# One-core local attention with an MLP on Trainium2: later buffers for the attention and new durations in its list schedule

## The chip, the cores and the metric

The kernel runs as one program on one core of a Trainium2 chip. The metric is the device time of one execution in microseconds. Engines are named as the profile names them: PE is TensorE (matmuls; PEld its weight loads), DVE is VectorE, ACT is ScalarE, POOL is GpSimd, SP is the engine whose queue issues every DMA here.

## The reference

```
q, k, v: (4, 8, 768, 64) float32
k_sum, v_sum = max over blocks of 32 of k, mean over blocks of 32 of v
scores = [ (q k^T)/8 where |i - j| < 16, else -1e9  |  (q k_sum^T)/8 + log 32 ]
a = exp(scores - rowmax); a = a / (sum + 1e-9)
attn = a @ [v | v_sum]                     (4, 8, 768, 64)
x = heads side by side                     (4, 768, 512)
xn = layernorm(x) * g_ln
out = x + relu(xn @ w_ch1) @ w_ch2         512 -> 2048 -> 512
```

## The kernel before

**The work.** The 3072 rows are 24 tiles of 128 (T); each tile's heads are two halves, so attention has 48 steps, t = 0 to 47, and the MLP works on 12 groups of two tiles (g). The first 12 steps (batch 0) run in float32 from K and V held whole on chip (tiles `k0_0` to `k0_3`, `qw0` to `qw5`, `vw0` to `vw5`; each step copies its window of K to `kx0` or `kx1`). The other 36 are "late" steps, in pairs of float16 numbers: `load_q` and `load_k` (lines 539 to 565) fetch q and the two halves of K (`ksg`), POOL puts the 24 block maxima beside the window, ACT makes the high half (`qhl`, `kh`) and DVE the low half (`kl`); `qk` multiplies on PE (`s`); `softmax` runs on DVE, POOL and ACT; `transp` (line 623) splits the probabilities (`p16`) and has a DMA transpose them (`pT`); `pv` multiplies with V on PE (`o`). Then `ln` and `lnT` normalize a tile and put it transposed into `xs`.

For each later batch, `batch_k`, `batch_q`, `batch_v` and `batch_s` read all of K, Q and V once more in pieces (staging tiles `bst`; in batch 1 `bst` and `qs` in turn) for maxima, sums and scales.

**The MLP.** The weights arrive as 32 pieces of 512 KB (`raw`); `dec_w` rebuilds each in three DVE operations (`wf`, `wf`, `raw`) and takes its squares on ACT, `scale_w` finds a scale from four or eight of them, `conv_w` splits each piece into a high half (ACT) and a low one (DVE), `wp`. Then `g1` (96 blocks, `h`, 24 matmuls each of 256 columns, read out by ACT as `hh` and by DVE as `hl`; two PSUM buffers for `h`) and `g2` (`a`, 512 columns).

**What sets the order.** Nothing is issued while the program is described. `Plan.record` keeps every operation with what it must follow; `Plan.schedule` is a list schedule over five in-order engines that uses a table of durations (`Plan.cost`), of waits between engines (`WAIT`, plus `slack`, a margin for some waits) and a simple model of the DMA queue; `Plan.improve` runs it forwards and backwards 32 times and keeps the order with the earliest end. `Plan.issue` then emits the operations in that order, all from one line, so every row of the profile says L321. Each engine runs its own list strictly in order, SP too: a DMA that must wait holds up all behind it.

**Buffers.** `work` gives a tile by its tag; a tag with one buffer must be let go by its last reader before the next tile of that tag is written. Before, `ksg` has one buffer (tag `qke`), `kh` one for each half, `qs`, `p16`, `pT` and `bst` one each. Two lines that the steps touch:

```python
ksg = work("qke", f"ksg{t}_{pr}", [P, 2, NC])
WAIT = dict(tensor=200, vector=140, scalar=160, gpsimd=90, sync=940)
```

Of the kernel before, what the change touches and what calls it, by code (L numbers as in the profile page):

```python
# [15 lines left out]
F16 = mybir.dt.float16  # L16
# [5 lines left out]
B, H, S, D = 4, 8, 768, 64  # L22
DM, DFF = 512, 2048
P = 128
# [5 lines left out]
NC = 184  # L30
# [25 lines left out]
LOADS = [("fetch_k0", 0), ("fetch_k0", 1), ("fetch_q", 0), ("gain",), ("fetch_blocks",), ("fetch_k0", 2), ("fetch_k0", 3)]  # L56
LOADS += [("fetch_v0", c) for c in range(7)] + [("fetch_tail", 0), ("fetch_q", 1), ("fetch_tail", 1), ("fetch_tail", 2)]
NV = 3
SLACK = 2500
SLACK2 = 800  # L60
WORDER = (
# [25 lines left out]
class Plan:  # L87
# [1 line left out]


    ENGINES = ("tensor", "vector", "scalar", "gpsimd", "sync")
    WAIT = dict(tensor=200, vector=140, scalar=160, gpsimd=90, sync=940)
    SAME = dict(tensor=0, vector=127, scalar=143, gpsimd=100, sync=0)
    ISSUE, SETUP, TICK, SWITCH, FIRST = 450, 650, 10240 / 3, 93, 3500

    def __init__(self):
        self.ops, self.slots, self.prev, self.uses = [], {}, {}, {}
        self.joined = False
        self.stages, self.stage = {None: 0}, 0
        for e in self.ENGINES:  # L100
            setattr(self, e, Plan.Queue(self, e))

# [7 lines left out]
    def step(self, f):  # L110


        def call(*a):
            outer, self.stage = self.stage, self.stages.setdefault((f.__name__, a), len(self.stages))
            f(*a)
            self.stage = outer

        return call
# [66 lines left out]
    def cost(self, engine, op, a, k, ins, outs):  # L185

        free = lambda x: math.prod(n for _, n in x.ap[1:])
        n = max(free(x) for x in ins + outs) if engine != "tensor" else free(a[0])
        if engine == "sync":
            x = (outs + ins)[0]  # L190
            return self.ISSUE, x.ap[0][1] * free(x) * mybir.dt.size(x.dtype) / (200.0 if "transpose" in op else 360.0)
        if engine == "tensor":
            dt = ins[-1].dtype
            if dt == F32R:
                return 0.443 * max(n, 256) + 4.5, 0.0
            if dt == F16 or op == "transpose":
                return max((1 if dt == F16 else 2) * n / 2.4 + 3.0, 28.0), 0.0
            return (2 if ins[0].ap[0][1] > D else 1) * max(2 * n / 2.4 + 2.0, 100.0), 0.0
        psum = any(x.space == bass.MemoryType.PSUM for x in ins)
        pointers = sum(1 for x in ins[1:] if free(x) == 1)  # L200
        if engine == "scalar":
            extra = ("accum_out" in k) + sum(isinstance(k.get(x), bass.AP) for x in ("scale", "bias"))
            return n / 1.2 + (51 if psum else 93) + 93 * extra, 0.0
        if engine == "vector":
            fixed = {"transpose": 183, "tensor_tensor_reduce": 158}.get(op, 70)
            return n / (1.92 if op == "tensor_scalar" and not psum else 0.96) + fixed + 61 * (pointers > 0), 0.0
        if op == "tensor_scalar":
            return 180 + n + 61 * pointers + 300 * (n == 1), 0.0
        if op == "tensor_copy":
            return 120 + 3.33 * n, 0.0  # L210
        if op == "tensor_tensor":
            shifted = outs[0].offset // outs[0].ap[0][0] != ins[0].offset // ins[0].ap[0][0]
            return 517 if n == 1 else 40 + 2.1 * n + 110 * (shifted or outs[0].dtype == F32R), 0.0
        return 60 + 0.8 * n, 0.0
# [7 lines left out]
        return engine == "vector" and (len(on_sbuf) > 1 or op == "tensor_scalar" and len(on_sbuf) == 1)  # L222

    def waits(self, x):
        e = [self.ops[j].engine for j in x.after]
        late = self.slack(x)
        return [(j, self.SAME[a] * y if a == x.engine else self.WAIT[a] + late) for a, (j, y) in zip(e, x.after.items())]

    def slack(self, x):

        name, a = self.names[x.stage]
        if x.engine != "tensor" or not a:
            return 0.0
        return SLACK * (name in ("qk", "pv", "batch_s")) + SLACK2 * (name in ("g1", "g2") and a[0] >= 24)

    def schedule(self, rank, after, back):

        count = len(self.ops)
        before = [[] for _ in range(count)]
        left = [len(x) for x in after]  # L240
        for i, x in enumerate(after):
            for j, wait in x:
                before[j].append((i, wait))
        ready, start, end = [0.0] * count, [0.0] * count, [0.0] * count
        free = dict.fromkeys(self.ENGINES, 0.0)
        coming, waiting = ({e: [] for e in self.ENGINES} for _ in range(2))
        ring, warm, columns, tick = 0.0 if back else self.FIRST, False, 0.0, 0.0
        port, half = 0.0, 0
        for i in range(count):
            if not left[i]:  # L250
                heapq.heappush(coming[self.ops[i].engine], (0.0 if back else 1000.0, i))
        for _ in range(count):
            t, e = min(
                (free[e] if waiting[e] else max(free[e], coming[e][0][0]), k)
                for k, e in enumerate(self.ENGINES)
                if waiting[e] or coming[e]
            )
# [12 lines left out]
            if e == "tensor" and not back:  # L270
                while t >= tick + self.TICK:
                    warm, columns, tick = columns >= 3200, 0.0, tick + self.TICK
                busy *= 1 if warm else 2
                at, per = t, self.ops[i].columns / busy
                while t + busy >= tick + self.TICK:
                    columns += (tick + self.TICK - at) * per
                    warm, columns, tick = columns >= 3200, 0.0, tick + self.TICK
                    at = tick
                columns += (t + busy - at) * per
            start[i], free[e], end[i] = t, t + busy, t + busy  # L280
            if e == "sync":
                ring = max(ring, t if back else t + busy + self.SETUP) + moving
                if back:
                    free[e] = max(free[e], ring)
                end[i] = ring + (self.SETUP + busy if back else 0)
            for j, wait in before[i]:
                ready[j] = max(ready[j], end[i] + wait)
                left[j] -= 1
                if not left[j]:
                    heapq.heappush(coming[self.ops[j].engine], (ready[j], j))  # L290
        return start, end
# [10 lines left out]
        return best  # L302

    def issue(self, nc):
        self.names = {n: k or ("", (0,)) for k, n in self.stages.items()}
        for x in self.ops:
            x.first = in_front(self.names[x.stage], x.engine)
        after = [self.waits(x) for x in self.ops]
# [5 lines left out]
        for i in reversed(range(len(after))):  # L314
            x = self.ops[i]
# [10 lines left out]
def body(ctx: ExitStack, tc, qt, qa, qe, kt, ks, va, vb, vs, g_ln, w1, w2, blocks, out):  # L326
# [5 lines left out]
    def work(tag, name, shape, dt=F32, bufs=1):  # L332
        return pl.tile(wp, shape, dt, tag, name, bufs)
# [23 lines left out]
    late = {}  # L357
# [41 lines left out]
    def go_late():  # L399
        nc.gpsimd.memset(prob[0][:, :, NC:], 0.0)  # L400
        for i in range(2):
            t = late["v", i] = work(f"v16_{i}", f"v16_{i}", [P, 2, 4, 2, D], F16)
            nc.gpsimd.memset(t[:], 0.0)

    stg_n = [0]

    def stg(tag, shape, dt=F32):
        stg_n[0] += 1
        if tag == "bst1":
            tag = ("bst", "qs")[stg_n[0] % 2]  # L410
        return work(tag, f"{tag}{stg_n[0]}", shape, dt, 1 + (tag == "xn"))


# [138 lines left out]
    def load_k(t, pr):  # L552
        T, hh = divmod(t, 2)
        b = T // NT
        ksg = work("qke", f"ksg{t}_{pr}", [P, 2, NC])
        nc.sync.dma_start(ksg[:], kt[T, hh, pr])
        nc.gpsimd.tensor_copy(
            ksg[:, :, 160 : 160 + NB], bt["k", b][:, 2 * hh + pr]
        )
        kh = work(f"kh{pr}", f"kh{t}_{pr}", [P, 2, NC], F16)  # L560
        kl = work("kl", f"kl{t}_{pr}", [P, 2, NC], F16, 2)
        sc = bt["s", b][:, 2:3]
        nc.scalar.activation(kh[:], ksg[:], AF.Copy, scale=sc)
# [59 lines left out]
    def transp(t):  # L623

        p = st[t, "p"]
        p16 = work("p2", f"p16_{t}", [P, 4, 3, P], F16)
        first, rest, last = (p16[:, :, i] for i in range(3))
        nc.scalar.copy(first, p[:, :, :P])
        nc.scalar.copy(last[:, :, :D], p[:, :, P:])
        nc.gpsimd.tensor_tensor(rest, p[:, :, :P], first, ALU.subtract)  # L630
        nc.gpsimd.tensor_tensor(last[:, :, D:], p[:, :, P:], last[:, :, :D], ALU.subtract)
        pT = work("pta", f"pT_{t}", [P, 12, P], F16)
# [440 lines left out]
```

## Time and profile before

| | |
|---|---|
| runs | 643.06, 643.38 and 646.51 us; median 643.38 us |
| the profiled execution | 640.14 us, of which 638.4 us from its first to its last instruction |
| PE busy | 609.2 us of 638.4 (95%), mean granted clock 0.989 |
| DVE, ACT, POOL busy | 454.4 (71%), 391.2 (61%), 198.7 us (31%) |
| DMA | 93.14 MB; the one queue's packets take 55.3% of 16 engines' span |

PE is in use nearly throughout, so what PE does not do (its idle time and the stretches at a lower granted clock) is all that an order can win. The sum of idle PE is 638.4 - 609.2 = 29.2 us; where it lies is read from a table by stretch, and what it waited for from the waits of that stretch.

### The profile page before, as it was taken

How to read it: one execution, taken by the hardware profiler on the slowest of the kernel's cores; microseconds unless marked ns; L12 is line 12 of the kernel's file. 1: busy time of each engine (PE TensorE's matmuls, PEld its weight loads, DVE VectorE, ACT ScalarE, POOL GpSimd, SP SyncE). 2: the span in 40 equal slices, each digit the busy share in tenths (PEclk: the TensorE clock that was granted, in tenths of full speed). 3: DMA queues.
4: the chain of work that ended last, by engine and by line, in shares of the span. 5: the costliest groups of instructions: out<-in, count | busy, mean ns of one | idle time of the engine just before them, and what ended most of it. 6: DMA issues, size and time to landing. Idle time of an engine off the chain costs nothing.

```text
span 638.4 us, 13412 instructions
## 1 busy us (share of the span) xinstructions
PE 609.2 (95%) x4611; PEld 430.7 (67%) x4611; DVE 454.4 (71%) x1190; ACT 391.2 (61%) x1036; POOL 198.7 (31%) x412
## 2 busy tenths in 40 slices
PE   8967999999989999899999999999999999999997
PEld 6845766664666776676676677776776766666665
DVE  4899989899678797677776788578776875432212
ACT  4989899678477775658667576565656664210100
POOL 5122110133343352363333545344344443200000
PEclk9979899999999999999999999999999999999999
DMA  9972476525967856678675675456665453420000
GB/s 287 351 270 70 128 260 213 192 83 124 237 162 179 194 138 162 174 160 195 176 145 149 152 170 114 111 132 150 153 147 140 113 149 75 62 51 1 17 16 34
DMA packets 124996, 93.14 MB, mean 146 GB/s; under 512 B 84864, under 2 KB 107392, under 8 KB 124928
## 3 DMA queue, kind: packets, MB, share of 16 engines
q1 hardware_dynamic: 124928, 92.29, 55.3%
q8 instruction: 36, 0.59, 0.4%
q14 instruction: 32, 0.26, 0.1%
HBM read 66.27 MB, written 6.29 MB: 114 GB/s over the span
## 4 chain that ended last, share of the span: by engine, by line
PE 42%; DVE 21%; DMA 20%; ACT 8%; issue 5%; SPq 2%; POOL 2%; ACTq 0%; POOLq 0%; DVEq 0%
PE h L321 19%; PE a L321 19%; DMA raw<-in_w 6%; DMA ksg<-in_kt 5%; DMA bst<-in_vs 4%; ACT p L321 3%; DVE p L321 2%; DVE wp L321 2%; DVE x L321 2%; DVE kl L321 2%; SPq L321 2%; DVE hl L321 2%; DMA bst<-in_ks 2%; PE s L321 2%; DVE wf L321 2%
## 5 line engine op out<-in xcount | busy, mean ns | idle before, releaser
L321 PE MATMUL h<-xs,wp 128*128 128x256 f16 x2304 | 274.8, 275 | 8.5 <-DVE hl L321 6.5
L321 PEld LDWEIGHTS <-wp 128*128 128x128 f16 x2304 | 225.5, 99 | 51.5 <-issue 8.6
L321 PE MATMUL a<-wp,hh 128*128 128x512 f16 (+1 forms) x768 | 226.7, 377 | 1.0 <-ACT hh L321 0.9
L321 PE MATMUL a<-wp,hl 128*128 128x512 f16 x384 | 144.9, 377 | 0.1
L321 PEld LDWEIGHTS <-hh 128*128 128x128 f16 x784 | 75.6, 98 | 68.0 <-ACT hh L321 1.1
L321 ACT ACTIVATE hh<-h 128x512 f16<-128x512 f32 x96 | 55.8, 584 | 88.6 <-PE h L321 88.2
L321 DVE SCALAR_TENSOR_TENSOR hl<-h,hh 128x512 f16<-128x512 f32 x96 | 65.3, 683 | 62.1 <-ACT hh L321 61.6
L321 ACT ACTIVATE p<-p,mn,sv 128x184 f32<-128x184 f32 x144 | 76.2, 530 | 22.2 <-POOL mn L321 21.7
L321 POOL TENSOR_TENSOR p<-p,p 128x512 f16<-128x512 f32 x72 | 70.1, 988 | 32.3 <-ACT p L321 32.1
L321 DVE SCALAR_TENSOR_TENSOR kl<-ksg,sv,kh 128x368 f16<-128x368 f32 x72 | 48.4, 672 | 30.9 <-ACT kh L321 30.8
L321 ACT ACTIVATE kh<-ksg,sv 128x368 f16<-128x368 f32 x72 | 42.9, 596 | 42.8 <-POOL ksg L321 37.2
L321 PEld LDWEIGHTS <-hl 128*128 128x128 f16 x392 | 38.3, 98 | 45.1 <-DVE hl L321 0.6
L321 ACT ACTIVATE bst<-bst 128x384 f32<-128x384 f32 (+2 forms) x55 | 32.3, 588 | 32.1 <-DVE vsum L321 15.1
L321 POOL TENSOR_SCALAR mn<-mn,sv 128x2 f32<-128x2 f32 x72 | 33.5, 466 | 56.0 <-DVE mn L321 55.6
L321 POOL COPY ksg<-ksum 128x48 f32<-128x48 f32 x72 | 19.1, 265 | 97.4 <-DMA ksg<-in_kt 90.0
L321 DVE SCALAR_TENSOR_TENSOR x<-a,wsc,x 128x512 f32<-128x512 f32 (+1 forms) x48 | 35.4, 737 | 18.4 <-PE a L321 18.3
L321 DVE CUSTOM_DVE_ANT_0 p<-s,mask 128x184 f32<-128x184 f32 x144 | 43.3, 340 | 1.4 <-PE s L321 1.4
L321 DVE SCALAR_TENSOR_TENSOR v<-vst,sv,v 128x256 f16<-128x256 f32 x72 | 36.6, 533 | 3.2 <-ACT v L321 2.9
L321 ACT CAST p<-p 128x512 f16<-128x512 f32 x72 | 33.9, 504 | 8.0 <-DMA pT<-p 7.7
L321 POOL TENSOR_TENSOR x<-x,rc 128x256 f32<-128x256 f32 x36 | 25.7, 715 | 40.5 <-DVE x L321 39.4
L321 ACT ACTIVATE v<-vst,sv 128x512 f16<-128x512 f32 x36 | 25.5, 712 | 11.5 <-PE o L321 11.5
L321 DVE SCALAR_TENSOR_TENSOR qhl<-qs,sv,qhl 64x512 f16<-64x512 f32 x36 | 28.2, 785 | 4.0 <-ACT qhl L321 2.9
(118 smaller groups left out, 767.6 us busy)
## 6 DMA issues: line engine op xcount, KB each, us to landing
raw<-in_w SPq DMA_DIRECT2D x32, 512.0 KB
ksg<-in_kt SPq DMA_DIRECT2D x72, 184.0 KB
qs<-in_qt SPq DMA_DIRECT2D x72, 128.0 KB
out_x<-x SPq DMA_DIRECT2D x23, 256.0 KB
vst<-in_va SPq DMA_DIRECT2D x36, 128.0 KB
bst<-in_ks SPq DMA_DIRECT2D x20, 192.0 KB
bst<-in_qa SPq DMA_DIRECT2D x15, 256.0 KB
bst<-in_vs SPq DMA_DIRECT2D x20, 192.0 KB
```

The costliest lines, as they stand in the source:

```text
L321: getattr(getattr(nc, self.ops[i].engine), op)(*a, **k)
```

## The change

Three things. **Homes:** late attention's tiles take tags in turn from a list, `HOMES`; the added tags are those of tiles that batch 0 is the last to use. `ksg` has three places in place of one, `kh` four in place of two, `qs`, `p16`, `pT` and `bst` two in place of one. **Durations:** the table gives a DMA's issue time by kind of step, a longer wait for its landing by kind of step, and other constants for several DVE, ACT, POOL and PE operations. **Margins:** `SLACK2` 800 becomes 1500 ns, and waits of ACT, DVE, POOL and SP in late attention get 1000 ns on what a DMA brings and 150 ns on the rest. Cut to its core:

```diff
+HOMES = dict(
+    ksg=("qke", "k0_0", "k0_1"),
+    kh=("kh0", "kh1", "kx0", "kx1"),
+    qs=("qs", "qw0"),
+    p16=("p2", "k0_2"),
+    pT=("pta", "k0_3"),
+    bst=("bst", "qw1"),
+)
-SLACK2 = 800
+SLACK2 = 1500
+SLACKD, SLACKE, LATE = 1000, 150, 14
...
-    ISSUE, SETUP, TICK, SWITCH, FIRST = 450, 650, 10240 / 3, 93, 3500
+    SETUP, TICK, SWITCH, FIRST = 1100, 10240 / 3, 93, 3500
+    ISSUE = dict(transp=1550, lnT=1250, batch_vput=760, load_q=500)
+    LAND |= dict(batch_q=1350, batch_v=1300, load_q=1350, load_v=1150, transp=1050)
...
-            return self.ISSUE, x.ap[0][1] * free(x) * mybir.dt.size(x.dtype) / (200.0 if "transpose" in op else 360.0)
+            return self.ISSUE.get(self.names[self.stage][0], 380), x.ap[0][1] * free(x) * mybir.dt.size(x.dtype) / (200.0 if "transpose" in op else 360.0)
...
+                wait.append((j, self.slack(x, y) + (self.LAND.get(n, 1000) if y.engine == "sync" else self.WAIT[y.engine])))
...
+        late = name in ("load_q", "load_k", "load_v", "softmax", "transp", "pv") and a[0] >= LATE
+        late |= name[:5] == "batch" and a[0] >= 2
+        late |= name in ("ln", "lnT") and a[0] >= LATE // 2
+        late |= name in ("g1", "g2") and a[0] >= 24
+        if not late:
             return 0.0
+        return SLACKD if y.engine == "sync" else SLACKE
...
-                ring = max(ring, t if back else t + busy + self.SETUP) + moving
+                ring = max(ring, t if back else t + self.SETUP) + moving
...
+    def home(kind):
+        n = turn[kind] = turn.get(kind, -1) + 1
+        return HOMES[kind][n % len(HOMES[kind])]
...
-        ksg = work("qke", f"ksg{t}_{pr}", [P, 2, NC])
+        ksg = work(home("ksg"), f"ksg{t}_{pr}", [P, 2, NC])
...
-        kh = work(f"kh{pr}", f"kh{t}_{pr}", [P, 2, NC], F16)
+        kh = work(home("kh"), f"kh{t}_{pr}", [P, 2, NC], F16)
```

No operation is added or taken away; their order changes on every engine. (The numbers after a name: `ksg20_0` is step 20, half 0; the last number is a running one.) Three places.

SP, where the K loads of steps 20 and 21 stand. Before:

```order
L321 DMA ksg20_0_688<-in_kt 128x368
L321 DMA_TRANSPOSE pT_18_633<-p16_18_632 128x12x128
L321 DMA vst1_78<-in_vb 32x256
L321 DMA vst1_78<-in_va 128x256
L321 DMA vst1_78<-in_vb 32x256
L321 DMA bst63_728<-in_vs 96x512
L321 DMA ksg20_1_691<-in_kt 128x368
L321 DMA qs66_755<-in_qt 64x512 x2
L321 DMA bst82_1051<-in_ks 128x384
L321 DMA ksg21_0_735<-in_kt 128x368
```

And of the change:

```order
L349 DMA ksg20_0_688<-in_kt 128x368
L349 DMA vst1_78<-in_vb 32x256
L349 DMA vst0_77<-in_vb 32x256
L349 DMA qw064_733<-in_qt 64x512 x2
L349 DMA qw161_726<-in_vs 96x512
L349 DMA ksg20_1_691<-in_kt 128x368
L349 DMA_TRANSPOSE pT_17_611<-p16_17_610 128x12x128
L349 DMA ksg21_0_735<-in_kt 128x368
L349 DMA vst0_77<-in_vb 32x256
L349 DMA_TRANSPOSE xs3_513<-x16_6_514 128x8x128
```

The load of `ksg20_0` stood beside the transpose of step 18 and now stands beside that of step 16; the loads run further ahead of the rest of attention.

ACT, from the read-out of block 24 of `g1` to that of block 26. Before:

```order
L321 ACTIVATE hh24_554<-h24_553 128x512
L321 ACTIVATE p_88,sum18_631<-p_88,mn18_630,sv1_435 128x184 x4
L321 CAST p16_18_632<-p_88 128x4x128
L321 CAST p16_18_632<-p_88 128x4x64
L321 ACTIVATE kh19_1_643<-ksg19_1_642,sv1_435 128x368
L321 ACTIVATE bst61_726,vabs2_704<-bst61_726 96x512
L321 ACTIVATE hh25_559<-h25_558 128x512
L321 ACTIVATE v16_1_262<-vst1_78,sv1_435 128x8x64
L321 ACTIVATE hh26_562<-h26_561 128x512
```

And of the change:

```order
L349 ACTIVATE hh24_554<-h24_553 128x512
L349 CAST p16_19_649<-p_88 128x4x128
L349 CAST p16_19_649<-p_88 128x4x64
L349 ACTIVATE bst62_727,vabs2_704<-bst62_727 96x512
L349 ACTIVATE qw163_728,vabs2_704<-qw163_728 96x512
L349 ACTIVATE kh21_1_739<-ksg21_1_738,sv1_435 128x368
L349 ACTIVATE hh25_559<-h25_558 128x512
L349 ACTIVATE qhl22_756<-qs66_755,sv1_435 128x512
L349 ACTIVATE v16_0_261<-vst0_77,sv1_435 128x8x64
L349 ACTIVATE kh22_0_758<-ksg22_0_757,sv1_435 128x368
L349 ACTIVATE p_88,sum20_697<-p_88,mn20_696,sv1_435 128x184 x3
L349 ACTIVATE hh26_562<-h26_561 128x512
```

The softmax beside these blocks was that of step 18 and is that of step 20; the K and q work is that of steps 21 and 22 where it was step 19. By block 47 this has grown: before, the `qk` of 16 steps (14 to 29) stand on PE between blocks 16 and 47 of `g1`; now 19 steps (14 to 32).

ACT, around the read-outs of blocks 2 and 3, early in the kernel (`tx3` is a transpose on PE whose copy, `xs1`, all of blocks 8 to 15 need). Before:

```order
L321 ACTIVATE hh2_302<-h2_301 128x512
L321 ACTIVATE bst10_414,vabs1_407<-bst10_414 128x384
L321 CAST xs1_191<-tx3_218 128x512
L321 ACTIVATE wf13_312,wacc_81<-raw13_276 128x512
L321 ACTIVATE wf14_313,wacc_81<-raw14_277 128x512
L321 ACTIVATE wf15_314,wacc_81<-raw15_278 128x512
L321 ACTIVATE hh3_305<-h3_304 128x512
```

And of the change:

```order
L349 ACTIVATE hh2_302<-h2_301 128x512
L349 ACTIVATE bst8_412,vabs1_407<-bst8_412 128x384
L349 ACTIVATE hh3_305<-h3_304 128x512
L349 CAST xs1_191<-tx3_218 128x512
L349 ACTIVATE qs9_413,vabs1_407<-qs9_413 128x384
L349 ACTIVATE bst10_414,vabs1_407<-bst10_414 128x384
L349 ACTIVATE wf16_342,wacc_81<-raw16_299,gcol_74 128x512
```

The copy of `tx3` was two rows behind `hh2` and ahead of `hh3`, and now follows `hh3`: on PE the transpose `tx3` stood between blocks 2 and 3, and now comes after block 3, directly ahead of a small scale matmul and block 8 (before, step 8's `qk` and block 9 came next).

## Rows read from the trace of the kernel before

**Rows 1.** The page, part 1: busy us (share of the span) and instructions of each engine.
```profile
PE 609.2 (95%) x4611; PEld 430.7 (67%) x4611; DVE 454.4 (71%) x1190; ACT 391.2 (61%) x1036; POOL 198.7 (31%) x412
```

**Rows 2.** Busy time by stretch: us, busy (count) by engine, granted clock, DMA share, GB/s.
```profile
32.00:64.00 32.00, 21.44 (x146) 16.91 (x143) 30.64 (x87) 28.42 (x92) 7.84 (x19) 0.85 0.49 171
64.00:96.00 32.00, 31.12 (x234) 23.63 (x233) 30.01 (x85) 29.55 (x90) 4.68 (x14) 0.94 0.62 194
...
160.00:192.00 32.00, 28.78 (x246) 21.31 (x245) 21.36 (x52) 19.82 (x50) 12.19 (x22) 1.00 0.76 198
192.00:256.00 64.00, 63.56 (x498) 44.02 (x497) 53.72 (x145) 44.12 (x115) 23.88 (x47) 1.00 0.71 169
256.00:320.00 64.00, 60.44 (x475) 42.12 (x474) 45.85 (x114) 42.95 (x115) 26.70 (x52) 1.00 0.72 176
320.00:384.00 64.00, 61.53 (x492) 44.19 (x491) 49.36 (x135) 43.00 (x109) 25.70 (x48) 1.00 0.66 154
384.00:512.00 128.00, 128.00 (x1053) 93.70 (x1052) 97.31 (x253) 80.97 (x196) 55.18 (x97) 1.00 0.58 134
```

**Rows 3.** Waits of PE, 160 to 384 us: us in total, times, longest.
```profile
PE h L321 <- DVE hl L321: 4.5, 5, 1.2
PE s L321 <- DVE kl L321: 1.9, 4, 0.7
PE h L321 <- DMA xs<-x: 1.5, 2, 0.8
PE a L321 <- ACT hh L321: 0.9, 1, 0.9
```

**Rows 4.** Waits of all engines in the same stretch.
```profile
POOL ksg L321 <- DMA ksg<-in_kt: 56.2, 30, 5.5
...
DVE vsum L321 <- DMA bst<-in_vs: 9.7, 8, 2.8
```

**Rows 5.** Waits of SP's queue in the same stretch.
```profile
SPq L321 <- DVE kl L321: 18.6, 16, 2.2
SPq L321 <- ACT bst L321: 16.6, 14, 3.9
```

**Rows 6.** Timeline of SP, 240 to 300 us: start, us, instruction.
```profile
239.66 1.66 SPq L321 DMA_TRANSPOSE pT<-p  x1
...
253.97 0.33 SPq L321 DMA_DIRECT2D ksg<-in_kt  x1
...
294.40 0.52 SPq L321 DMA_DIRECT2D ksg<-in_kt  x1
...
297.94 2.05 SPq L321 DMA_TRANSPOSE pT<-p  x1
```

**Rows 7.** Timeline of POOL, the same stretch; in brackets the idle time before.
```profile
256.36 0.53 POOL L321 COPY ksg<-ksum 128x48 f32<-128x48 f32 x1 [0.65 <-DMA ksg<-in_kt]
...
298.19 0.22 POOL L321 COPY ksg<-ksum 128x48 f32<-128x48 f32 x1 [1.67 <-DMA ksg<-in_kt]
```

**Rows 8.** Timeline of DVE, 28 to 64 us.
```profile
45.39 1.88 DVE L321 SCALAR_TENSOR_TENSOR raw<-raw,wf 128x512 uint32<-128x512 uint32 x3
47.19 0.54 DVE L321 TENSOR_REDUCE kmax<-bst 128x12 f32<-128x384 f32 x1
```

**Rows 9.** Timeline of PE, 42 to 76 us; in brackets the idle time before.
```profile
50.50 0.88 PE L321 MATMUL pp<-ident,p 128*128 128x128 f32 x3 [1.60 <-ACT p L321]
...
62.91 5.15 PE L321 MATMUL h<-xs,wp 128*128 128x256 f16 x24
68.03 0.63 PE L321 MATMUL tx<-ident,xn 128*128 128x128 f32 x4
68.50 2.78 PE L321 MATMUL h<-xs,wp 128*128 128x256 f16 x24
...
73.14 1.47 PE L321 MATMUL h<-xs,wp 128*128 128x256 f16 x12 [0.52 <-DVE wsc L321]
```

**Rows 10.** Timeline of DVE, 66 to 72 us.
```profile
70.67 0.68 DVE L321 TENSOR_TENSOR xs<-tx,xs 128x512 f16<-128x512 f32 x1
```

More of the change, by code (lines that the diff above doesn't have):

```diff
@@ L91 @@
     ENGINES = ("tensor", "vector", "scalar", "gpsimd", "sync")
-    WAIT = dict(tensor=200, vector=140, scalar=160, gpsimd=90, sync=940)
+    WAIT = dict(tensor=200, vector=140, scalar=160, gpsimd=90, sync=1000)
     SAME = dict(tensor=0, vector=127, scalar=143, gpsimd=100, sync=0)
-    ISSUE, SETUP, TICK, SWITCH, FIRST = 450, 650, 10240 / 3, 93, 3500
+    SETUP, TICK, SWITCH, FIRST = 1100, 10240 / 3, 93, 3500
+    ISSUE = dict(transp=1550, lnT=1250, batch_vput=760, load_q=500)
+    LAND = dict(fetch_v0=2050, fetch_k0=1950, fetch_q=2000, fetch_w=1750, fetch_tail=2000, gain=2000)
+    LAND |= dict(batch_q=1350, batch_v=1300, load_q=1350, load_v=1150, transp=1050)
     def __init__(self):
@@ L98, in __init__ @@
         self.joined = False
-        self.stages, self.stage = {None: 0}, 0
+        self.names, self.stage = [("", ())], 0
         for e in self.ENGINES:
@@ L113, in call @@
         def call(*a):
-            outer, self.stage = self.stage, self.stages.setdefault((f.__name__, a), len(self.stages))
+            outer, self.stage = self.stage, len(self.names)
+            self.names.append((f.__name__, a))
             f(*a)
@@ L197, in cost @@
                 return max((1 if dt == F16 else 2) * n / 2.4 + 3.0, 28.0), 0.0
-            return (2 if ins[0].ap[0][1] > D else 1) * max(2 * n / 2.4 + 2.0, 100.0), 0.0
+            return max(2 * n / 2.4 + 2.0, 100.0) * 2 if ins[0].ap[0][1] > D else 2 * n / 2.4 + 53.0, 0.0
         psum = any(x.space == bass.MemoryType.PSUM for x in ins)
@@ L202, in cost @@
             extra = ("accum_out" in k) + sum(isinstance(k.get(x), bass.AP) for x in ("scale", "bias"))
-            return n / 1.2 + (51 if psum else 93) + 93 * extra, 0.0
+            weights = self.names[self.stage][0] in ("dec_w", "conv_w")
+            return n / 1.2 + (51 if psum else 93) + 93 * extra + 35 * weights, 0.0
         if engine == "vector":
-            fixed = {"transpose": 183, "tensor_tensor_reduce": 158}.get(op, 70)
-            return n / (1.92 if op == "tensor_scalar" and not psum else 0.96) + fixed + 61 * (pointers > 0), 0.0
+            fixed = {"tensor_tensor_reduce": 78, "reciprocal": 90}.get(op, 70) + 61 * pointers
+            fixed += 119 * (self.box(ins[0])[1] == D)
+            return n / (1.92 if op == "tensor_scalar" and not psum else 0.96) + fixed, 0.0
         if op == "tensor_scalar":
-            return 180 + n + 61 * pointers + 300 * (n == 1), 0.0
+            return 180 + n + 61 * pointers + 90 * (n == 1), 0.0
         if op == "tensor_copy":
-            return 120 + 3.33 * n, 0.0
+            return 60 + 3.33 * n, 0.0
         if op == "tensor_tensor":
@@ L224, in waits, with slack @@
     def waits(self, x):
[L225 to L229, printed above, removed]
-        name, a = self.names[x.stage]
-        if x.engine != "tensor" or not a:
+        wait = []
+        for j, real in x.after.items():
+            y = self.ops[j]
+            if y.engine == x.engine:
+                wait.append((j, self.SAME[x.engine] * real if x.engine != "sync" or real else None))
+            else:
+                n = self.names[y.stage][0]
+                wait.append((j, self.slack(x, y) + (self.LAND.get(n, 1000) if y.engine == "sync" else self.WAIT[y.engine])))
+        return wait
+    def slack(self, x, y):
+        name, a = self.names[x.stage]
+        if x.engine == "tensor":
+            if name in ("g1", "g2"):
+                return SLACK2 * (a[0] >= 24)
+            return SLACK * (name in ("qk", "pv", "batch_s"))
+        late = name in ("load_q", "load_k", "load_v", "softmax", "transp", "pv") and a[0] >= LATE
[3 more added lines that the diff above has]
+        if not late:
             return 0.0
-        return SLACK * (name in ("qk", "pv", "batch_s")) + SLACK2 * (name in ("g1", "g2") and a[0] >= 24)
+        return SLACKD if y.engine == "sync" else SLACKE
     def schedule(self, rank, after, back):
@@ L281, in schedule @@
             if e == "sync":
-                ring = max(ring, t if back else t + busy + self.SETUP) + moving
+                ring = max(ring, t if back else t + self.SETUP) + moving
                 if back:
                     free[e] = max(free[e], ring)
-                end[i] = ring + (self.SETUP + busy if back else 0)
+                end[i] = ring + (self.SETUP if back else 0)
             for j, wait in before[i]:
-                ready[j] = max(ready[j], end[i] + wait)
+                ready[j] = max(ready[j], free[e] if wait is None else end[i] + wait)
                 left[j] -= 1
@@ L304, in issue @@
     def issue(self, nc):
-        self.names = {n: k or ("", (0,)) for k, n in self.stages.items()}
         for x in self.ops:
@@ L403, in go_late @@
             nc.gpsimd.memset(t[:], 0.0)
+    turn = {}
+    def home(kind):
+        n = turn[kind] = turn.get(kind, -1) + 1
+        return HOMES[kind][n % len(HOMES[kind])]
     stg_n = [0]
@@ L410, in stg @@
             tag = ("bst", "qs")[stg_n[0] % 2]
+        elif tag in ("bst", "qs"):
+            tag = home(tag)
         return work(tag, f"{tag}{stg_n[0]}", shape, dt, 1 + (tag == "xn"))
@@ L625, in transp @@
         p = st[t, "p"]
-        p16 = work("p2", f"p16_{t}", [P, 4, 3, P], F16)
+        p16 = work(home("p16"), f"p16_{t}", [P, 4, 3, P], F16)
         first, rest, last = (p16[:, :, i] for i in range(3))
@@ L631, in transp @@
         nc.gpsimd.tensor_tensor(last[:, :, D:], p[:, :, P:], last[:, :, :D], ALU.subtract)
-        pT = work("pta", f"pT_{t}", [P, 12, P], F16)
+        pT = work(home("pT"), f"pT_{t}", [P, 12, P], F16)
         nc.sync.dma_start_transpose(pT[:], p16.rearrange("p j i k -> p (j i k)"))
```

## The prediction

> **What bounds the kernel now.** I began with the busy shares: PE works 609.2 us of the span of 638.4 [rows 1], so nothing but the 29.2 us of idle PE, and time at a lower granted clock, can be won by an order. The table by stretch then says where they lie [rows 2]. Idle PE is the stretch less PE's busy time: 10.56 us in 32 to 64, 0.88 in 64 to 96; then 3.22, 0.44, 3.56 and 2.47 in the four stretches from 160 to 384, together 9.69; and none in 384 to 512. The reader should see two different limits. Up to 96 us DVE is busy 30.64 and 30.01 of 32 us: it rebuilds and splits the weights, PE waits for it, and the granted clock is 0.85 and 0.94. From 160 to 384 us no engine but PE is full (DVE 45.85 of 64 in 256 to 320) and the clock is 1.00; PE still stops.
>
> What it stops for is in its waits of that stretch [rows 3]: low halves of the MLP (`h` for `hl`) 4.5 us, low halves of K (`s` for `kl`) 1.9, `xs` 1.5, `hh` 0.9: 8.8 of the 9.69. `kl` and `hl` are short DVE operations, and DVE is no more than 84% busy there, so they are late because DVE or ACT stood, in order, behind something that had not come. The waits of all engines name it [rows 4]: POOL waits 56.2 us, 30 times, for the one `ksg` buffer's load, at worst 5.5, and DVE 9.7 us for `bst` (8 times). And why the loads are late is in SP's waits [rows 5]: 18.6 us, 16 times, until `kl` has let go of `ksg`, and 16.6 us until ACT has let go of `bst`.
>
> So late attention is a circle: the next K load is issued only when the last `kl` is done, and lands too late for the next. The planner did not see it. By its constants, a K load is ready at 450 + 650 + 523 (188 KB at 360 a ns) + 940 = 2.56 us after its start on SP. The trace has 253.97 to 256.36 = 2.39 for one and 294.40 to 298.19 = 3.79 for another [rows 6, 7].
>
> **The change, part by part.** It adds and removes no operation, so the sum is made of PE's idle time.
>
> *Homes.* With three places for `ksg` and two for `bst`, a load waits for a reader three (or two) tiles back. The 18.6 and 16.6 us of SP's waits go, in the main; PE does not gain these, only what of them came through as its 9.69 us.
>
> *Durations and margins.* A K load is now planned as 1.10 + 0.52 + 1.00 + 1.00 (margin) = 3.62 us. That covers the first measured landing (2.39) by far and the second (3.79) nearly. So what is late next is a landing above 3.6 us, and those are a minority.
>
> What is left of the 9.69 us: nothing, at the best. At the worst everything. The nearest row is a stretch of the same kind in which the plan held: 192 to 256 us lost 0.44 in 64 us, which is 1.5 over the 224 us. I double it to 3, because attention becomes denser (19 `qk` between blocks 16 and 47 of `g1` where 16 stood). **Late term: 9.7 to 3, gain 6.7 (bounds 0 to 9.7)**.
>
> *SP's queue.* All loads and transposes are its work. In 240 to 300 us it ran 61 issues from 239.66 to 297.94 (the first and the last of them: [rows 6]), 42.6 us in sum, 71%. Denser by 19/16 this is 84%; the DMA engines go from 0.72 to some 0.86. Neither is full, so I cost it at nothing; the cover is the margin of 1 us on each landing, and if that is gone it is the first rival.
>
> *The early part.* The margins don't touch it, the new durations and homes do.
> (a) Transpose `tx3` now follows block 3 in place of block 2. Its copy `xs1` is what block 8 needs, and PE has only small work between. In the trace the transpose ends at 68.66 and DVE's `xs1` at 70.67 + 0.68 = 71.35 [rows 9, 10]: hidden then, by block 3's 2.78 us. Uncovered it costs at least DVE's 0.68 and at most 2.69; I take 1.6, near the middle, since `hh3` now goes ahead of ACT's cast.
> (b) Up to the last conversion that block 2 waits for, the new DVE order has two more `raw` rebuilds (1.88 / 3, less overlap: 0.60 each [rows 8]), two more `wf` operations (0.5 each, an estimate below the 0.60 of `raw`), and two fewer `kmax` (0.54 [rows 8]) and a small one: +1.2 + 1.0 - 1.1 = +1.1. DVE is full, so this reaches PE.
> (c) Half of block 1 (12 of its 24 matmuls, 2.78 / 2 = 1.4) now stands ahead of step 6's probability transposes, `pp`, where PE idled 1.60 us [rows 9]: -1.4.
> (d) Block 9's wait for `wsc`, 0.52 [rows 9], may go, as DVE is a little ahead by then: -0.5.
> **Early term: 1.6 + 1.1 - 1.4 - 0.5 = about +1**. Bounds: without the gains of (c) and (d) and with 2.69 for (a), +3.8; with 0.68 for (a) and nothing for (b), -1.2. One thing widens the lower side: block 2 ran its 24 matmuls in 5.15 us, block 3 in 2.78 at full clock [rows 9], after PE had idled; if these idle gaps close, 2.4 us come back, so -3.6.
>
> *After 384 us* nothing is idle to win (128.00 of 128), and from block 84 of `g1` on PE's order is the same: 0.
>
> **Sum:** -6.7 + 1 = -5.7; 640.14 becomes 634.4 for an execution like the profiled one. The median of the runs shown is 643.38, 3.24 above the profiled one; I keep that distance: **637.7 us**. A half per cent, 3.2 us, is about what a measurement of this kernel can tell from no change.
>
> **The rivals.**
>
> *Slower: landings stretch with the density.* Loads are issued earlier and closer together, transposes among them, and each lands later; if the usual landing passes 3.6 us, the margins are used up and K is late at nearly every step, not at four. The price of one is the mean of PE's waits for `kl`, 1.9 / 4 = 0.48 us [rows 3]: 19 steps x 0.48 = 9.1 where 1.9 stood, the other waits stay: +7.2, with the early +1 it is 643.4 + 8.2 = 651.6. For it speaks that two loads of one kind within 45 us already differ by 1.4 us [rows 6, 7], and that the slower lands beside a transpose of 2.05 us. Against it: in 160 to 192 us the DMA share was highest, 0.76, and 192 to 256 at 0.71 was nearly clean [rows 2]. It decides when DMA share passes what the trace has seen (0.76). The Trainium skill, page "DMA: Bandwidth & Descriptors", section "Latency and other measured facts", gives the access time of the memory as 0.2 us on average and 2 us at high load; by that rule all of the spare 1.2 us of a landing of 2.39 could be eaten, and the time would be this rival's. The two landings here, 2.39 and 3.79, differ by less than the page's 1.8 us; no run so far shows the load at which they grow.
>
> *No change: the stalls move.* The 8.8 us of named waits are mostly `hl`, not K; if DVE falls behind because more attention is now pressed into the same blocks (if half of its 45.85 of 64 is attention, an estimate, 19/16 of that half makes 50), half of the late gain goes: -3.3; the early term at its upper end, +3.8: +0.5, 643.9. For it: the same in-order engines, and more work between the read-outs on ACT, as its order shows (eleven operations between `hh24` and `hh26` where nine stood).
>
> *More: all of it.* The late 9.7 gone and the early part at -2 (clock regained): 631.7. For it speaks only that the lower bounds are reachable; every term must go well.
>
> *It does not do what it says.* The new homes `k0_0` and `k0_1` are read until batch 0's last windows are copied. A `ksg` load placed there ahead of a weight piece `raw` on SP would hold the weights up if the copies were late. Two such loads do stand ahead of weight pieces. The weights are wanted by a DVE that is full until 96 us, so a late piece would cost PE directly; I give it no chance of its own and count it to the slower case.
>
> **How the numbers follow.** Forecast (634 to 640.2): 0.47. More (below 634): 0.13. No change (640.2 to 646.6): 0.25. Slower (above 646.6): 0.15. So faster 0.60, same 0.25, slower 0.15. The likeliest is the forecast, 637.7. The range reaches down to "more", 631.7, and up through "no change" to 646.6: left out are about 0.05 below and 0.15 above.
>
> **What would show it.** Right: SP's waits for `kl` and `bst` below a third of 18.6 and 16.6; POOL's wait for `ksg` well below 56.2; PE idle in 160 to 384 at about 3, with `h` for `hl` below 1.5; a new wait of PE for `xs1` near 70 us, some 1.6. Wrong: a DMA share above 0.8 with PE's waits for `kl` at more than ten steps (the slower rival), or SP's waits gone and PE's waits for `hl` still 4 us (no change: then the cause was DVE's order, not the loads), or idle PE before 96 us up by more than 4.

## The result, and the profile after

| | before | changed |
|---|---|---|
| median | 643.74 us (643.06 to 646.51, 4 runs) | 638.01 us (636.59 to 638.30, 4 runs) |
| ratio | | 0.9886, 95% interval 0.9861 to 0.9912 |
| profiled execution, its span | 640.14, 638.4 us | 638.03, 636.2 us |

1.1% faster. One warning ahead of all reading of traces: the profiled execution of before was one of its quickest (in the 17, 35 and 17 runs beside the experiments, on three chips, before lay between 639.97 and 649.82 us), that of the changed kernel is its median. Between the two traces only 638.4 - 636.2 = 2.2 of the 5.7 us can be seen.

The page's first part, of the changed kernel:

```profile
PE 610.9 (96%) x4611; PEld 433.3 (68%) x4611; DVE 450.8 (71%) x1190; ACT 391.5 (62%) x1036; POOL 207.8 (33%) x412
```

Idle PE is 636.2 - 610.9 = 25.3 us where it was 29.2 [rows 1]: 3.9 less. PE is busy 1.7 us longer, though it does the same work: some of it at half clock (1.2 GHz in place of 2.4). By stretch (columns as in [rows 2]):

```profile
32.00:64.00 32.00, 21.50 (x144) 17.28 (x144) 31.38 (x91) 28.84 (x89) 6.21 (x15) 0.85 0.48 158
64.00:96.00 32.00, 30.33 (x216) 23.11 (x215) 28.18 (x73) 26.77 (x76) 7.80 (x16) 0.89 0.65 209
96.00:160.00 64.00, 63.27 (x435) 42.26 (x435) 62.24 (x162) 54.69 (x151) 15.91 (x31) 1.00 0.56 164
160.00:192.00 32.00, 32.00 (x266) 23.54 (x265) 23.67 (x68) 26.99 (x74) 14.96 (x28) 1.00 0.93 233
192.00:256.00 64.00, 62.13 (x510) 44.46 (x508) 59.34 (x164) 49.54 (x128) 34.56 (x60) 1.00 0.78 187
256.00:320.00 64.00, 63.76 (x529) 45.57 (x526) 54.96 (x139) 51.23 (x137) 35.78 (x58) 1.00 0.86 206
320.00:384.00 64.00, 60.40 (x480) 43.48 (x479) 54.83 (x154) 44.13 (x110) 30.38 (x55) 0.97 0.66 153
```

From 160 to 384 us PE's idle time is now 0, 1.87, 0.24 and 3.60, in sum 5.71 for 9.69 [rows 2]: 4.0 less. DVE and ACT are busier there (DVE 54.96 of 64 in 256 to 320, where it had 45.85), as more attention is done in the same time, and the DMA share in that stretch is 0.86 for 0.72. In 32 to 64 us idle PE is 10.50 for 10.56; in 64 to 96 us 1.67 for 0.88, and the clock 0.89 for 0.94.

PE's waits from 160 to 384 us, of the changed kernel (us in total, times, longest):

```profile
PE h L349 <- DVE hl L349: 3.4, 1, 3.4
PE h L349 <- DMA xs<-x: 1.6, 1, 1.6
```

Two lines of all engines' waits in that stretch:

```profile
POOL ksg L349 <- DMA ksg<-in_kt: 32.9, 21, 4.0
...
DVE p L349 <- POOL p L349: 10.0, 8, 2.2
```

And three of SP's:

```profile
SPq L349 <- POOL mn L349: 26.8, 14, 4.0
...
SPq L349 <- DVE kl L349: 6.5, 11, 1.6
...
SPq L349 <- ACT bst L349: 1.8, 4, 0.6
```

Five short waits for `hl` [rows 3] have become one of 3.4 us, and the waits for `kl` are gone. SP waits 6.5 us for `kl` where it waited 18.6, and 1.8 us for ACT's `bst` where it waited 16.6 [rows 5]; POOL waits 32.9 us for K where it waited 56.2 [rows 4]. There are new waits: DVE's for POOL's reading of `p`, 10.0 us, and SP's of 26.8 us ahead of the transposes of `p`, put down to POOL's `mn`.

**The one long stall that is left.** PE's timeline around it, in the changed kernel:

```profile
329.83 1.15 PE L349 MATMUL h<-xs,wp 128*128 128x256 f16 x9
334.42 2.74 PE L349 MATMUL h<-xs,wp 128*128 128x256 f16 x12 [3.44 <-DVE hl L349]
...
337.84 1.47 PE L349 MATMUL h<-xs,wp 128*128 128x256 f16 x12
```

DVE's:

```profile
328.11 1.10 DVE L349 SCALAR_TENSOR_TENSOR kl<-ksg,sv,kh 128x368 f16<-128x368 f32 x2
331.29 0.35 DVE L349 CUSTOM_DVE_ANT_0 p<-s,mask 128x184 f32<-128x184 f32 x1 [2.08 <-POOL p L349]
...
333.69 0.68 DVE L349 SCALAR_TENSOR_TENSOR hl<-h,hh 128x512 f16<-128x512 f32 x1
```

POOL's, and then SP's, where the K load was issued:

```profile
327.17 0.22 POOL L349 COPY ksg<-ksum 128x48 f32<-128x48 f32 x1 [3.12 <-DMA ksg<-in_kt]
...
328.02 2.21 POOL L349 TENSOR_TENSOR p<-p,p 128x512 f16<-128x512 f32 x1
...
330.59 0.67 POOL L349 TENSOR_TENSOR p<-p,p 128x256 f16<-128x256 f32 x1
```
```profile
312.58 1.44 SPq L349 DMA_TRANSPOSE pT<-p  x1
...
323.64 1.32 SPq L349 DMA_DIRECT2D ksg<-in_kt  x2
```

Read it from the bottom. SP had no gap over 0.11 us between its issues from 312.58 until the K load at 323.64. POOL waited 3.12 us for it, so it began late to read step 30's `p`, and took 2.21 us for the first part of it; the second part ended at 331.26. DVE stood 2.08 us before step 31's softmax, which writes the one `p`. The `hl` of block 43, whose input was there at 330.2, stood behind that in DVE's order until 333.69, and PE for 3.44 us. Then come 12 matmuls in 2.74 us, at a mean granted clock of 0.56 (1.2 GHz for the most part), where the same 12 take 1.47 us at full clock (2.4 GHz): between 334.42 and 337.90 the lower clock takes another 3.48 x (1 - 0.56) = 1.5 us.

Of POOL's 2.21 us, 1.10 are the time of two `kl` operations of DVE that began just then. Without them, 1.11 are left, beside the 1.16 that the operation mostly takes elsewhere in this trace. The Trainium skill, "SBUF — State Buffer", section "SBUF: two separate sides", says that VectorE and GpSimd share a port pair as an exclusive lock, which a VectorE operation with two SBUF inputs takes too, and that the first to start keeps it. The trace agrees in the length; in the order it doesn't show the rule, since POOL's row begins 0.09 us before DVE's.

### The profile page after: what moved, and what is told of

Its sections match the earlier page's. It is cut to its first block, busy times and chain, and to the rows that moved or that the text cites. A ratio compares the mean times of both kernels' runs of the same rounds, so it can differ in the third digit from the quotient of the medians.

```text
span 636.2 us, 13437 instructions
## 1 busy us (share of the span) xinstructions
PE 610.9 (96%) x4611; PEld 433.3 (68%) x4611; DVE 450.8 (71%) x1190; ACT 391.5 (62%) x1036; POOL 207.8 (33%) x412
## 4 chain that ended last, share of the span: by engine, by line
PE 52%; DVE 25%; DMA 8%; ACT 6%; POOL 4%; issue 4%; SPq 1%; DVEq 0%; ACTq 0%; POOLq 0%
PE a L349 23%; PE h L349 23%; DVE x L349 3%; DVE p L349 3%; DMA ksg<-in_kt 3%; DVE wf L349 2%; ACT p L349 2%; PE o L349 2%; DVE hl L349 2%; PE s L349 2%; POOL p L349 2%; DVE qhl L349 2%; DVE kl L349 2%; DVE v L349 2%; DVE wp L349 1%
## 5 line engine op out<-in xcount | busy, mean ns | idle before, releaser
L349 PE MATMUL h<-xs,wp 128*128 128x256 f16 x2304 | 278.2, 276 | 6.7 <-DVE hl L349 4.8
L349 POOL TENSOR_TENSOR p<-p,p 128x512 f16<-128x512 f32 x72 | 72.3, 1010 | 35.0 <-ACT p L349 33.2
L349 DVE CUSTOM_DVE_ANT_0 p<-s,mask 128x184 f32<-128x184 f32 x144 | 42.2, 343 | 16.6 <-POOL p L349 10.0
L349 DVE SCALAR_TENSOR_TENSOR kl<-ksg,sv,kh 128x368 f16<-128x368 f32 x72 | 44.5, 643 | 3.3 <-PE s L349 3.2
L349 DVE SCALAR_TENSOR_TENSOR v<-vst,sv,v 128x256 f16<-128x256 f32 x72 | 40.4, 588 | 2.3 <-ACT v L349 2.0
L349 POOL COPY ksg<-ksum 128x48 f32<-128x48 f32 x72 | 24.3, 338 | 47.9 <-DMA ksg<-in_kt 44.5
L349 DVE TENSOR_REDUCE x<-o 128x256 f32<-128x512 f32 x36 | 24.6, 685 | 16.2 <-PE o L349 15.9
L349 PEld LDWEIGHTS <-qhl 128*128 128x128 f16 x288 | 24.4, 99 | 5.2 <-issue 0.3
```

What stands on the lines that cost most here:

```text
L349: getattr(getattr(nc, self.ops[i].engine), op)(*a, **k)
```

## The experiments

All ratios are to the kernel before on the same chip, with 95% intervals; e1 to e4, e5 to e8 and e9 to e12 each shared a chip, so between these groups ratios are compared, not times. *Planned again* means that the list schedule ran on the edited program. *Fixed order* means that it did not run: each engine gets the rows of an earlier kernel, in that order, word for word.

```diff
-        best = self.improve(rank, after, then, ROUNDS)
-        for _, i in sorted(zip(best[1], range(len(after)))):
+        for i in self.fixed(after):
```

(`fixed` yields the operations in an order that is written into the file.) For fixed orders the code is that of the changed kernel, so that no wait differs but those for places.

### e1: the homes alone, planned again

The kernel before, with `HOMES` and `home` of the change; table and margins old.

> Homes alone, planned again with the old durations and margins. Theory A (the late stalls are K and batch loads that come too late; homes let them start early, the durations and margins make the plan count on their true landing; each gives a part): SP's waits for kl (18.6 us before) fall below 8, but loads are still planned as landing after 2.56 us; about half of the late idle of 9.69 us goes, 3 us off the kernel before: ratio 0.993 to 0.998. Rival B (the table of durations alone does it): ratio 0.998 to 1.004. Rival C (the homes alone do all of it): 0.986 to 0.991.

Measured: 639.97 us (12 runs), ratio 0.9963 (0.9937 to 0.9989). Theory A's number, and its reading of the trace holds: SP waits 6.1 us for `kl`. But idle PE from 160 to 384 us is 5.56 us, as low as with the whole change; in this execution the plan's belief in 2.56 us cost nothing there. It is the quickest of the twelve (637.15 us, 2.8 below their median), so what this order loses at the median is not in its trace. One stretch is worse than before: idle PE in 32 to 64 us is 12.11, for 10.56 [rows 2].

### e2: durations and margins alone, every place single

```diff
-    ksg=("qke", "k0_0", "k0_1"),
+    ksg=("qke",),
```

and the other five lines likewise.

> Durations and margins alone, every place single as before. Theory A: the plan now knows that a K load on a single place is late and puts other work ahead of it, but the loads still wait: SP's waits for kl stay above 12 us, half of the late idle goes, ratio 0.993 to 0.999. Rival B (the table does it): 0.986 to 0.991. A third way: with the wider margins on single places attention is pushed behind and PE waits more, ratio above 1.002.

Measured: 668.89 us, 1.0388 (1.0359 to 1.0417): the third way, which had only a lower bound, 1.002. PE's waits of the whole execution, of e2, say where:

```profile
PE h L342 <- DMA xs<-x: 13.7, 5, 4.2
```

The MLP now waits for its own input, 13.7 us, as attention runs behind: DVE is still busy 67.31 us in 512 to 640 us, where e3 has 42.59. That is a part of the loss: idle PE is 43.4 us in all for 25.3 in the changed kernel, and the mean granted clock 0.964 for 0.984.

### e3: the old order, row for row, with the homes

> The kernel before's order, row for row on every engine, with the new homes: only the waits for places go. Theory A1 (the loads' start is what was late): SP's waits for kl fall from 18.6 to below 5, POOL's for ksg from 56.2 to below 35, PE's idle time in 160 to 384 us from 9.69 to about 5, ratio 0.991 to 0.995. Rival D (in a fixed order SP is held by its other waits, so K loads start hardly earlier): POOL's wait for ksg above 45, late idle above 8, ratio 0.998 to 1.002.

Measured: 636.76 us (635.74 to 637.40), 0.9898 (0.9874 to 0.9921). Within the intervals this is all that the whole change gives, with no new duration, margin or order. SP's waits from 160 to 384 us, of e3:

```profile
SPq L435 <- ACT v L435: 21.1, 7, 5.0
...
SPq L435 <- DVE kl L435: 2.4, 2, 2.2
...
SPq L435 <- ACT bst L435: 0.6, 2, 0.4
```

The first of these three lines, before:

```profile
SPq L321 <- ACT v L321: 2.0, 3, 1.2
```

From the waits of all engines, of e3:

```profile
POOL ksg L435 <- DMA ksg<-in_kt: 49.2, 22, 5.4
```

And the stretches:

```profile
160.00:192.00 32.00, 29.51 (x246) 21.48 (x245) 21.20 (x56) 20.44 (x55) 12.14 (x24) 1.00 0.80 216
192.00:256.00 64.00, 64.00 (x504) 44.67 (x503) 54.20 (x143) 44.69 (x115) 24.59 (x47) 1.00 0.69 172
256.00:320.00 64.00, 61.30 (x482) 42.71 (x480) 48.30 (x120) 43.71 (x118) 27.29 (x54) 1.00 0.76 180
320.00:384.00 64.00, 64.00 (x521) 46.48 (x520) 51.77 (x140) 44.41 (x112) 28.14 (x50) 1.00 0.63 152
```

SP's waits for `kl` and for ACT's `bst` fall from 18.6 and 16.6 [rows 5] to 2.4 and 0.6, and PE's idle time to 2.49 + 0 + 2.70 + 0 = 5.19 us. Yet POOL still waits 49.2 us for K, as rival D had it: K comes hardly earlier on the whole. SP's waiting has moved: it now stands 21.1 us for ACT to let go of V's staging tile (2.0 before). So the queue gets past the held loads and stands at later ones; that PE's gain comes by what was behind those loads is argued, not shown.

### e4: the changed kernel's order with a second `p`

```diff
-    ksg=("qke", "k0_0", "k0_1"),
+    ksg=("qke", "k0_0", "qw2"),
...
+        prob.append(work("k0_1", "p3", [P, 4, NE]))
...
-        st[t, "p"] = prob[t < NEARLY and t % 2]
+        st[t, "p"] = prob[t % 2 * (1 if t < NEARLY else 2)]
```

> The changed kernel's order, row for row (one small memset more), but late attention's tile p in two places in turn (the place of k0_1; the third ksg place moves to that of qw2). Theory E (what is left is the one p: DVE waited 10.0 us, 8 times, for POOL to have read it, and the stall of 3.44 us at 331 with the half clock behind it, 1.5 us, hangs on this): DVE's waits for POOL p fall below 3, the stall goes, about 5 us off the changed kernel: 633, ratio 0.980 to 0.985. Rival F (POOL itself is late: its subtraction took 2.2 us there where 1.2 is usual, and what waits for its rs and mn stays late): the stall stays above 2 us, ratio 0.987 to 0.991 like the changed kernel.

Measured: 635.94 us (632.03 to 637.49), 0.9876 (0.9844 to 0.9908). Rival F. DVE's waits for `p` are gone, but the stall is still 2.81 us, since a row of DVE's order between softmax and `hl` waits for POOL as well. DVE's timeline, of e4:

```profile
331.38 0.83 DVE L435 TENSOR_SCALAR xn<-x,mv,rs 128x512 f32<-128x512 f32 x1 [1.62 <-POOL rs L435]
```

### e5 and e6: the old order, and one half of the homes

e5 has the new places of `ksg` and `kh` alone, e6 those of `bst` and `qs` alone; the rest is single.

> The kernel before's order, row for row, with new places for ksg and kh alone. Theory A2 (the K loads' wait for kl, 18.6 us on SP, is the larger part of the 6.5 us that all homes gave at this order): ratio 0.990 to 0.994, PE's late idle about 6 us. Rival G (the batch pieces are: SP stands before a bst load until ACT let go of the last, and everything behind it on SP is late): 0.996 to 1.001, late idle above 8 us, SP's waits for ACT bst still above 12 us.

> The kernel before's order with a second place for bst and qs alone. Theory A2: ratio 0.996 to 1.000, SP's waits for kl still above 12 us. Rival G: 0.990 to 0.994, SP's waits for ACT bst below 4 us and late idle about 6. If both e5 and this give under a third of the 6.5 us, the two circles only open together.

Measured: e5 641.05 us, 0.9968 (0.9938 to 0.9997); e6 639.53 us, 0.9925 (0.9903 to 0.9947). Both halves count, and 0.32% and 0.75% add up to 1.07%, beside e3's 1.02%. By the ratios the batch pieces are the larger part, against A2, but the two intervals overlap, and in the stretch that the homes are for the halves are alike: from 160 to 384 us PE idles 7.36 us in e5 and 7.53 in e6 (9.69 before, 5.19 in e3). As all four traces have the same rows in the same order, one can also follow them from one matmul to another: from the `g2` matmul that begins at 160.12 us before to the `g1` matmul at 384.03 PE takes 223.9 us before, 221.0 in e5, 221.2 in e6 and 217.9 in e3. SP's waits from 160 to 384 us, of e5:

```profile
SPq L428 <- ACT bst L428: 23.2, 18, 4.3
SPq L428 <- POOL ksg L428: 15.6, 10, 3.5
```

And of e6:

```profile
SPq L428 <- DVE kl L428: 31.4, 20, 3.3
SPq L428 <- DVE mn L428: 16.8, 13, 3.9
```

With one circle open SP stands longer in the other: for `bst` 23.2 us (16.6 before), or for `kl` 31.4 us (18.6 before).

### e7 and e11: the new durations without the new margins

```diff
-SLACK2 = 1500
-SLACKD, SLACKE, LATE = 1000, 150, 14
+SLACK2 = 800
+SLACKD, SLACKE, LATE = 0, 0, 14
```

e7 with the homes, e11 with single places; both planned again.

> The changed kernel with its homes and durations, planned again with the old margins (800 ns for g1 and g2, none for late attention's other engines). Theory H (with the homes the true durations are enough, the margins add nothing measurable): ratio 0.986 to 0.993, within 2 us of the changed kernel's 638.0. Rival I (the margins are what covers K loads that land 1 us above the mean): PE's late idle above 8 us, ratio 0.995 to 1.003.

> The new durations, every place single, the old margins. It tells what made e2 (new durations and new margins on single places) 668.9. Theory N (the margins did: with one place, 1 us more on each landing is paid at every load, so attention falls behind): 640 to 647. Rival O (the new durations themselves did, as they say that a single place cannot keep up): above 655.

Measured: e7 642.58 us, 0.9993 (0.9967 to 1.0020), rival I; its idle PE from 160 to 384 us is 1.41 + 2.68 + 4.94 + 0 = 9.03. e11 644.04 us, 0.9980 (0.9956 to 1.0003), theory N. So with the new durations the margins are worth -1.1% where places rotate, and cost +4.1% where each is single.

### e8: second `p`, planned again

> The changed kernel with two places for late attention's p, and the order planned anew with them (e4 had the changed kernel's order: 635.9). Theory J (the plan can use the second p: softmax of a step no longer follows POOL's reading of the last, so attention moves further ahead): late idle below 4 us, 632 to 635, ratio 0.982 to 0.987. Rival K (another order has other accidents on POOL and SP, which is 84% busy between 256 and 320 us): 636 to 641, ratio 0.988 to 0.997.

Measured: 642.14 us, 0.9974 (0.9951 to 0.9996). Rival K, worse than its number: this order has an accident of its own, in which PE waits 4.2 us at once for DVE's `mn`, a part of the softmax; and PE idles 19.73 us up to 160 us, where the changed kernel has 16.37.

### e9 and e10: the stall at 331 us, by one row

In e9, `fixed` gets five more edges, so that on DVE `hl` of block 43 (operation 1683) goes ahead of the softmax of step 31 and what follows it; in e10, which has e4's second `p` too, it gets one, `xn` behind `hl`. All other rows stay.

```diff
+        for b in (2089, 2286, 1893, 2072, 2027):
+            then[1683].append(b)
+            left[b] += 1
```

> The changed kernel with its own order, but one row moved on DVE: hl of block 43 now stands ahead of the softmax of step 31 instead of 12 rows behind it. Theory L (the stall of 3.44 us at 331 is DVE standing in order: the softmax waited 2.08 us for POOL, which had waited 3.12 us for a K load, and hl, ready since 330.2, stood behind it): the stall falls below 0.5 us and the half clock behind it (1.5 us) goes; about 5 us, 633. Rival M (what stood behind moves on: step 31's softmax is 0.6 us later, and hl of block 44 or K of step 32 is late instead): 636 to 639.

> As e4 (the changed kernel's order, two places for p), and on DVE xn of tile 13 moved behind hl of block 43, two rows on: in e4 that hl stood behind xn, which waited 1.62 us for POOL's rs. Theory L: the stall of 2.81 us and 1.5 us of half clock go, 635.9 becomes 631 to 632.5. Rival M: 634 to 637.

Measured: e9 636.61 us (633.06 to 640.58), 0.9863 (0.9825 to 0.9901); e10 635.42 us (632.35 to 637.63), 0.9843 (0.9811 to 0.9875). The changed kernel on the same chip is e12, 0.9872. Neither can be told from it. DVE's timeline at the place, of e9:

```profile
331.08 1.87 DVE L438 SCALAR_TENSOR_TENSOR kl<-ksg,sv,kh 128x368 f16<-128x368 f32 x2
333.12 0.69 DVE L438 SCALAR_TENSOR_TENSOR hl<-h,hh 128x512 f16<-128x512 f32 x1 [0.17 <-ACT hh L438]
```

And PE's waits after 160 us:

```profile
PE h L438 <- DMA xs<-x: 1.8, 1, 1.8
PE o L438 <- DMA pT<-p: 1.7, 1, 1.7
```

`hl` runs 0.17 us after its input came, and the stall with its half clock is gone (the clock of 320 to 384 us is 1.00). So theory L has its mechanism right. But not all of its time is won: PE now waits 1.7 us for a `pT` at 339.00, behind the softmax that was moved. From 320 to 384 us 2.00 us of idle PE are left, where e12 has 3.00. The measured time is rival M's; but between 160 and 320 us this execution had 4.32 us of idle PE where e12's had 1.96, and as the rows up to there are the same in both, this is not the edit's doing. A gain of 1 or 2 us would be hidden in such differences. In e10 the stall was still 2.30 us.

### e12: the changed kernel again

> The changed kernel once more, on the chip of e9 to e11, so that they can be compared with it: 637 to 639.

Measured: 637.24 us (634.57 to 639.68), 0.9872 (0.9837 to 0.9907).

### The four corners

The two entries of 1 are the kernel before itself.

| ratio to before | single places | homes |
|---|---|---|
| the order of before, fixed | 1 | 0.9898 (e3) |
| planned, old durations and margins | 1 | 0.9963 (e1) |
| planned, new durations, old margins | 0.9980 (e11) | 0.9993 (e7) |
| planned, new durations and margins | 1.0388 (e2) | 0.9886, 0.9872 (changed, e12) |

## Why the prediction was right, and where not

**The number** was right: 637.7 forecast, 638.0 measured, and the sign with it. Its terms were not all, and that they met to 0.3 us is in part luck: from trace to trace -5.7 us was forecast, and -2.2 came (the last point).

- *The circle* was the cause: late attention waits for its own places. e3 shows it, as only the waits for places differ there, and 1.0% goes. e5 and e6 show that it has two halves, the K loads and the batch pieces, of which neither does it alone.
- *The late term was mis-sized*: 9.7 to 3 was said, 5.71 was measured, so 4.0 and not 6.7 us in the traces. The forecast doubled what a clean stretch left; what stayed was mostly one stall of 3.44 us, which the chain K load, POOL, `p`, DVE makes of the denser attention. I had looked for what is late next among the landings above 3.6 us. This K load was issued at 323.64 and its copy on POOL ran at 327.17, 3.53 us after, inside the planned 3.62. What was late was its issue, in an SP queue without gaps, and behind it stood POOL's and DVE's rows in order. Nor had the forecast a term for the half clock behind a stall, 1.5 us here.
- *The step that failed* is "Durations and margins". I let them share the gain. With the old order and the homes the time is the same as with all three parts (0.9898 beside 0.9886 and 0.9872). Planning again with the homes loses 0.65% (e1) or 0.95% (e7) against the old order; the margins win that back, and no more that could be measured.
- *The early term* (+1) came out near, but not by its parts. Idle PE up to 160 us was 16.21 us and is 16.37. PE's timeline there, of the changed kernel:

```profile
45.51 1.09 PE L349 MATMUL tx<-ident,xn 128*128 128x128 f32 x4 [5.48 <-DVE xn L349]
...
53.30 0.82 PE L349 MATMUL pp<-ident,p 128*128 128x128 f32 x6
...
61.75 0.90 PE L349 MATMUL pp<-ident,p 128*128 128x128 f32 x3 [2.37 <-ACT p L349]
...
73.89 0.28 PE L349 MATMUL h<-xs,wp 128*128 128x256 f16 x1 [1.35 <-DVE hl L349]
74.48 6.96 PE L349 MATMUL h<-xs,wp 128*128 128x256 f16 x47 [0.31 <-DVE xs L349]
```

  And two lines of before:

```profile
42.37 1.08 PE L321 MATMUL tx<-ident,xn 128*128 128x128 f32 x4 [4.76 <-DVE xn L321]
...
61.58 0.79 PE L321 MATMUL o<-vst,pT 128*128 128x128 f32 x2 [2.07 <-ACT pT L321]
```

  (c) was right: `pp` runs without the gap of 1.60 [rows 9]. (d) was right, the wait for `wsc` is gone. (a) came in size: PE waits 1.35 for an `hl` that DVE runs right ahead of the copy, and then 0.31 for `xs` itself, 1.66 in sum beside my 1.6. But this wait has a half clock behind it that I had not counted: the 47 matmuls take 6.96 us, where 24 take 2.78 at full clock [rows 9] and 47 would take 5.4, so 1.5 more. (b) may be what shows in the wait of `tx` for `xn`, 5.48 us where it was 4.76; it was not tried alone. The wait of 2.37 for ACT's `p` I had not named; it stands where `o` waited 2.07 for ACT's `pT`. Idle time and this half clock together would make the early part 1.7 us worse from trace to trace. As PE's busy time is only 1.7 us longer in all, some of the 1.5 us each of the two half clocks comes back elsewhere; where, is not shown.
- *SP and the DMA queue* went as said on the mean: SP's issues of 256 to 320 us, 79 in 71 rows of its timeline, sum to 53.7 us, 84% (the 61 of the forecast were such rows too). But I costed this at nothing, and where SP ran without a gap the K load of the stall stood in it; the DMA share from 256 to 320 us is 0.86, and the slower rival's point of decision, 0.76, was passed. Landings did stretch, by less than it asked for. From SP's issue to the copy on POOL that waited for the load, K loads of 160 to 384 us took 2.35 to 4.44 us before (30 of them, median 2.83) and 2.63 to 5.02 after (22, median 3.05). By the records of their packets in the traces, a K load's last packet ended 2.2 us after its issue in the median before (38 loads) and 2.5 after (47). Six of the 22 took more than the planned 3.62; none of these is the load of the stall. The rule of the Trainium skill that I had set against the change ("DMA: Bandwidth & Descriptors", "Latency and other measured facts") did not decide here: the usual landing grew by 0.2 to 0.3 us, and PE's waits for `kl` are gone.
- *The distance* of 3.24 us between the profiled execution and the median was kept as a constant, and that was luck too: it is 0 for the changed kernel. In the traces the change is worth 2.2 us, in the medians 5.7. Where before's trace was quick can be seen, as e3, e5 and e6 have its rows in its order: the `g2` matmul that begins at 160.12 us in it begins at 162.71, 164.07 and 163.50 in theirs. So the quick execution was 2.6 to 3.9 us ahead early, where the homes have little to do yet (all K loads but one start at 132 us or later), and beside a usual execution of before the changed kernel's early part need not be worse at all. Why executions differ there stays open, and so does what else the slower executions of before lose: that is in no trace here.

Open as well: whether the homes of `p16` and `pT` give anything. They weren't tried alone; e5 and e6 already add up to e3, but their intervals are 0.2 to 0.3% wide on either side.

No version beat the changed kernel clearly. e3 does as well with the old order, and e10 has the lowest ratio, 0.9843, inside the changed kernel's intervals.

## What to carry to other kernels

Where in-order queues load into a single place, look at what the *queue* waits for, not only at what the compute engine waits for: rotating over dead tiles was worth 1.0% with not one row moved. To find out what part of a re-planned kernel's gain is the plan, fix the old order and change only the buffers; here the plan's share was too small to measure. In this kernel, margins on a wait helped only where a buffer stood behind them: the same margins (1 us on what a DMA brings) that recovered 1.1% with rotating places cost 4.1% with single ones.

## What the runs showed that was not expected

A stall can cost more than its length: behind 3.44 us of idle PE at 331 us came 3.5 us at a mean granted clock of 0.56, 1.5 us more, and behind 1.66 us at 72 to 74 us, in a stretch where PE had idled before too, another 1.5. Shorter stalls did it in one run and not in another: behind e10's 2.30 us the mean granted clock from 333 to 337 us was 0.66, behind e9's 1.72 us at 339 it stayed at 1.00. And planning the same operations anew moves the time by more than most edits: with the homes in place four orders gave 0.9898, 0.9963, 0.9993 and 0.9872.
